# Turning the first two chunks of x on TensorE instead of in the DMA

## The chip, the cores and the metric

The kernel runs on one core of one Trainium2 chip. The metric is the device time of one execution in microseconds (us). The core has five engines that this document names: TensorE (PE in the profile, with PEld for its weight loads), VectorE (DVE), ScalarE (ACT), GpSimd (POOL) and SyncE (SP), whose queue issues almost all DMA transfers.

## What is computed

The input x has 2048 tokens of 640 numbers in bfloat16. A linear attention with 32 heads of 20 numbers (branch a) and a gated feed-forward layer of width 1728 (branch b) are both computed from x, and a gate for each token mixes them:

```python
g = _sigmoid((x * gate_w).sum(-1, keepdims=True))
a = _A_ref(x, A_wqkv, A_w_phi, A_wo)          # heads, softmax features, num / den, @ wo
b = (_silu(x @ w_gate) * (x @ w_up)) @ w_down
return g * a + (1 - g) * b
```

The change concerns only how the first quarter of x reaches the products `x @ w_gate` and `x @ w_up`.

## The kernel before, in words

**Tiling.** The tokens are worked on in four blocks of 512. The 640 columns of x are five chunks of 128. TensorE sums over the partitions, so x is kept transposed in `xT`: chunk, then token, with the 128 columns of a chunk on the partitions. The feed-forward width is cut into 14 tiles k (13 of 128 columns and one of 64); one tile of a block is a group of five matmuls for gate and five for up, 512 tokens wide, one for each chunk. `wg` and `wu` hold the gate and up weights.

**Order.** The code does not issue instructions in the order in which it is written. It hands tasks to a plan (`_Plan`, L241), each with an engine, an assumed cost, what it depends on, a priority and the PSUM banks that it takes and frees. The plan's `run` (L286) simulates time with these figures: whenever an engine is free, the task of the best priority whose dependencies have ended is issued. A load's end is the due time `land` that its call gives. Some tasks of the later stages also have a `hold`, a fixed simulated time before which they do not start (`K_AT`, `Q_AT`, `PRE_AT`, L724 to L727). The result is one fixed instruction order for each engine; on the chip, semaphores make each instruction wait for its data.

**The loads.** `load` (L494) chains all transfers of SyncE's queue in the order of the calls. The first are, L547 to L553: gate weights of chunks 0 and 1 for the tiles k = 0 to 3 (256 KB), x chunks 0 and 1 of the first 512 tokens through the DMA's transpose, the up weights of chunks 0 and 1, gate weights of chunks 2 to 4 for k = 0 and 1, x chunks 2 and 3 and then 4 (transposed), and the rest of the weights for k = 0 to 3. After them come the next columns of gate and up, and the second block of x.

**The head.** TensorE begins with ten 512-column warm-up matmuls on constants (`warm`, L618; instructions at L623), whose results nobody reads. They are chained in front of `ffn_head` (L694), which treats the tiles k = 0 to 3 of the first block in an order by arrival of data: gate for chunks 0 and 1 (eight matmuls), up for chunks 0 and 1 (eight), then chunks 2 to 4 of gate (twelve) and of up (twelve). All these matmuls are issued at L450, in the helper `mms`; copies from PSUM by ScalarE and its other functions are at L460, DMA issues at L478, memsets at L470. ScalarE, VectorE and GpSimd finish each tile (`ffn_tail`: L460, L665, L671). The plan fills the time in which the attention's chain is not ready with further tiles of the feed-forward layer.

Of the kernel before, what the change touches and what calls it, by code (L numbers as in the profile page):

```python
# [6 lines left out]
P = 128  # L7
S_TOK = 2048
D = 640
H = 32  # L10
DH = 20
F_FFN = 1728
NT = S_TOK // P
# [16 lines left out]
NPC_W = 6  # L30
PHI_NH = (6, 6, 6, 6, 6, 2)
ACTF = mybir.ActivationFunctionType
ALU = mybir.AluOpType
AX = mybir.AxisListType
DT = mybir.dt
BF16 = DT.bfloat16
# [204 lines left out]
class _Plan:  # L241
# [11 lines left out]
    def add(self, eng, cost, fn, deps=(), prio=5.0, lat=None, acq=(), rel=(), name=""):  # L253
        t = _Task(eng, cost, fn, deps, prio, self.LAT[eng] if lat is None else lat,
                  tuple(acq), tuple(rel), len(self.tasks), name)
        self.tasks.append(t)
        return t
# [82 lines left out]
def _mm(*cols):  # L340
    return sum(c / 2400.0 + 0.003 for c in cols)


def _build(
# [13 lines left out]
    pe, act, dve, pool, sp = nc.tensor, nc.scalar, nc.vector, nc.gpsimd, nc.sync  # L358
    run = tr.run

    def rowelems(shape):
        r = 1
        for s_ in shape[1:]:
            r *= s_
        return r

    def sb(name, shape, dtype):
        t = nc.alloc_sbuf_tensor(name, list(shape), dtype)
        tr.reg_tensor(t, "sbuf", nc.lookup_mloc(t).addr, rowelems(shape), mybir.dt.size(dtype))
        return t  # L370

    def sbat(name, shape, dtype, at):
        t = nc.alloc_sbuf_tensor_at(name, list(shape), dtype, offset=at)
        tr.reg_tensor(t, "sbuf", at, rowelems(shape), mybir.dt.size(dtype))
        return t

    xT = sb("xT", [P, 5, S_TOK], BF16)
# [33 lines left out]
    base = nc.lookup_mloc(slab).addr  # L411
# [2 lines left out]
    wqT = sbat("wqT", [P, 2 * NPC_W, D], BF16, base)  # L414
    wbd = sbat("wbd", [P, NPC_W, 6, DH], BF16, base + 2 * NPC_W * D * 2)
    wph = sbat("wph", [PC, NPC_W, DH], BF16, base + 2 * NPC_W * D * 2 + NPC_W * 6 * DH * 2)

    ps = nc.alloc_psum_tensor("ps", [P, 8 * 512], F32)
    tr.addr[ps.name] = ("psum", 0, 8 * 512, 4)

    x2 = A_x[0]
# [3 lines left out]
    add = plan.add  # L425
# [4 lines left out]
    def one(b, c0, c1, r0=0, r1=P):  # L430
        return ps[r0:r1, b * 512 + c0:b * 512 + c1]
# [4 lines left out]
    def mms(groups):  # L436

        reads = [g[1] for g in groups] + [g[2] for g in groups]
        writes = []
        seen = set()  # L440
        for g in groups:
            k = (g[0].offset, str(g[0].ap))
            if k not in seen:
                seen.add(k)
                writes.append(g[0])

        def fn():
            last = None
            for o, l, r, st, sp_ in groups:
                last = pe.matmul(o, lhsT=l, rhs=r, start=st, stop=sp_, skip_group_check=True)  # L450
            return last
        run("pe", fn, reads=reads, writes=writes)
# [5 lines left out]
    def actop(o, i, func, scale=1.0):  # L458
        reads = [i] + ([scale] if isinstance(scale, bass.AP) else [])
        run("act", lambda: act.activation(o, i, func, scale=scale), reads=reads, writes=[o])  # L460

    def dveop(fn, reads, writes):
        run("dve", fn, reads=reads, writes=writes)

    def poolop(fn, reads, writes):
        run("pool", fn, reads=reads, writes=writes)

    def memset(t_ap, val, eng):
        eobj = {"pool": pool, "dve": dve}[eng]
        run(eng, lambda: eobj.memset(t_ap, val), reads=[], writes=[t_ap])  # L470
# [3 lines left out]
    def dma(eng, dst, src, transpose=False, keep=False):  # L474
        eobj = tr.engobj[eng]
        reads = [src] if src.tensor.name in tr.addr else []
        writes = [dst] if dst.tensor.name in tr.addr else []
        fn = (lambda: eobj.dma_start(dst, src, transpose=True)) if transpose else (lambda: eobj.dma_start(dst, src))  # L478
        ev = run(eng, fn, reads=reads, writes=writes, semname="dma")
        if keep:  # L480
            out_evs.append(ev)
# [12 lines left out]
    def load(eng, dst, src, land, prio, transpose=False, name="load", cost=0.06):  # L494

        t = add(eng, cost, lambda: dma(eng, dst, src, transpose=transpose), prio=prio, lat=2.0, name=name)
        t.land = land
        t.slack = L_SLACK if land > 13 else 0.0
        t.after = chain.get(eng)
        chain[eng] = t  # L500
        return t
# [7 lines left out]
    wgl = [None] * (NPC + 1)  # L509
    wul = [None] * (NPC + 1)  # L510

    def load_gu(j, eng, land, prio):
        c0, c1 = PIECES[j]
        wgl[j] = load(eng, wg[:, :, c0:c1], gsrc[:, :, c0:c1], land[0], prio)
        wul[j] = load(eng, wu[:, :, c0:c1], usrc[:, :, c0:c1], land[1], prio + 0.1)

    def load_x(bt, prio, *cuts):

        tok = slice(512 * bt, 512 * bt + 512)
        out_ = []  # L520
        for i, (c0, c1, land) in enumerate(cuts):
            out_ += [load("sp", xT[:, c0:c1, tok], x2[tok, c0 * P:c1 * P], land, prio + 0.1 * i, True, "x%d" % bt)] * (c1 - c0)
        return out_
# [13 lines left out]
    xs = [None] * NBT  # L537
    HD = 4
    hw = {}

    def load_head(key, c0, c1, k0, k1, land, prio):
        w, src = (wg, gsrc) if key == "g" else (wu, usrc)
        t = load("sp", w[:, c0:c1, k0 * P:k1 * P], src[:, c0:c1, k0 * P:k1 * P], land, prio)
        for k in range(k0, k1):
            hw[key, c0, k] = t
        return t
    load_head("g", 0, 2, 0, HD, 3.9, -43)  # L547
    xa = load_x(0, -42, (0, 2, 5.25))
    load_head("u", 0, 2, 0, HD, 6.9, -41)
    load_head("g", 2, 5, 0, 2, 7.4, -40.5)  # L550
    xs[0] = xa + load_x(0, -40, (2, 4, 8.8), (4, 5, 9.3))
    wgl[0] = load_head("g", 2, 5, 2, HD, 10.0, -39.5)
    wul[0] = load_head("u", 2, 5, 0, HD, 11.3, -39)  # L553
    load_gu(1, "sp", (12.5, 13.7), -37)
    xs[1] = load_x(1, -36.5, (0, 5, 16.4))
    phi_rows = A_w_phi.rearrange("h e f -> (h e) f")
# [16 lines left out]
    xl = [x_[4] for x_ in xs]  # L573

    zero = add("dve", 0.3, lambda: memset(us[:, 0, 0:2], 0.0, "dve"), prio=-20, name="zero")
    table = add("act", 1.3, lambda: actop(us[:, 1, 0:1], us[:, 0, 0:1], ACTF.Tanh), deps=[zero], prio=-20, name="table")
# [39 lines left out]
    def warm(banks, before):  # L618
        ctx = {}

        def fn():
            for b in banks:
                last = pe.matmul(one(b, 0, 512), lhsT=ones_row[:, 0:P], rhs=ones_row[:, 0:512], start=True, stop=True, skip_group_check=True)  # L623
            return last
        b0, b1 = min(banks), max(banks) + 1
        t = add("pe", 0.427 * len(banks), lambda: run("pe", fn, reads=[], writes=[ps[:, b0 * 512:b1 * 512]]), prio=-10,
                acq=[("bank", ctx, i) for i in range(b0, b1)], rel=[("bank", ctx, i) for i in range(b0, b1)], name="warm")
        t.after = before
        return t
    warm_t = warm((4, 5, 6, 7, 4, 5), warm((0, 1, 2, 3), None))  # L630


    gate_t = {}
# [60 lines left out]
    def ffn_head():  # L694
        tsl = slice(0, 512)
        cs = [{} for _ in range(HD)]
        before = warm_t
        last = {}

        def group(key, c0, c1, parts):  # L700
            nonlocal before
            w = wg if key == "g" else wu

            def fn(ks, cc):
                mms([(one(cs[k][key], 0, 512), w[:, c, P * k:P * k + P], xT[:, c, tsl], c == 0, c == 4) for c in cc for k in ks])
            for ks in parts:
                t = add("pe", _mm(*[512] * (len(ks) * (c1 - c0))), lambda ks=ks: fn(ks, range(c0, c1)),
                        deps=[xs[0][c1 - 1], hw[key, min(c0, 2), ks[-1]]], prio=-5,
                        acq=[("bank", cs[k], key) for k in ks] if c0 == 0 else (), name="head")
                t.after = before  # L710
                before = t
                for k in ks:
                    last[key, k] = t
        group("g", 0, 2, [(0, 1, 2, 3)])
        group("u", 0, 2, [(0, 1, 2, 3)])
        group("g", 2, 4, [(0, 1)])
        group("g", 4, 5, [(0, 1)])
        group("g", 2, 5, [(2, 3)])
        group("u", 2, 5, [(0,), (1,), (2,), (3,)])
        for k in range(HD):  # L720
            ffn_tail(0, k, cs[k], (last["g", k], last["u", k]), 0)
# [372 lines left out]
    pre_q = premult(0, wqT_l, PRE_Q, 0.02)  # L1094
    wq_done[0] = pre_q[-1]
    ffn_head()
    for bt in range(NBT):
        for t in range(4 * bt, 4 * bt + 4):
# [5 lines left out]
    for bt in range(1, NBT):  # L1104
        ks = list(range(K_PAIRS if bt == 1 else 0, NK))
# [74 lines left out]
```

## Time and profile before

| What | Value |
|---|---|
| median of 3 runs | 286.7 us (286.43 to 286.81) |
| the profiled execution | 286.7 us, of which the span of its instructions is 285.0 us |
| first warm-up matmul, first real matmul | 0.84 us, 5.10 us |
| a 512-column matmul of the real work, mean duration of one | 379 to 381 ns; they overlap, the next starts after 0.216 us |
| first weights: issue, landing | 0.80 us, 3.0 us later |
| transposed x chunks 0 and 1: issue, landing | 1.31 us, 3.6 us later |
| busy share of the 16 DMA engines, 3 to 8 us, for each microsecond | 0.96 to 1.27 |
| ScalarE idle before its first copy of the head | 8.3 us, until 10.57 |

Times in the profile count from the start of the span. A line of the timeline gives the start, the length, the engine, the line of the kernel, the instruction with the names of the tiles that it writes and reads, and in brackets how long the engine was idle before it and what ended that. Successive matmuls overlap in the record, so their pace is read from the starts, and the starts of the weight loads are the finest view of it. A queue's line (SPq) shows the issuing of a transfer, not its landing.

### The profile page before, as it was taken

The page shows a single profiled execution, that of the slowest core. Times are in us where ns is not written, and L with a number is a line of the kernel's source. Part 1 is how long each engine was busy: PE and PEld are TensorE (multiplying, and loading weights), DVE is VectorE, ACT ScalarE, POOL GpSimd, SP SyncE. Part 2 cuts the span into 40 slices and gives each one's busy share as a digit, 9 for nine tenths or more (in the row PEclk, how much of TensorE's full clock was granted, in tenths as well). Part 3 has the DMA queues.
Part 4 walks back from the last instruction along what each step waited for, and adds up shares of the span by engine and source line. Part 5 has one row for each costly group of instructions (what it writes and reads, how often), then busy time and mean ns, then how long its engine had stood idle before and what let it go on. Part 6 is the DMA issues. An engine that isn't in the chain of part 4 may idle for free.

```text
span 285.0 us, 4720 instructions
## 1 busy us (share of the span) xinstructions
PE 281.9 (99%) x1816; PEld 143.4 (50%) x1816; DVE 225.8 (79%) x326; ACT 150.2 (53%) x242; POOL 172.4 (61%) x170
## 2 busy tenths in 40 slices
PE   8999999999999999999999999999999999999996
PEld 3445554555554544555455455455555554554544
DVE  1323449998999797997999999999998989982132
ACT  2455655886676564345761655366655454563210
POOL 5099633749478637366498286588888643867100
PEclk9999999999999999999999999999999999999999
DMA  7979998940000000000002344444344544535211
GB/s 169 264 124 232 231 234 121 307 140 0 0 2 0 2 18 0 2 0 18 2 1 54 74 97 92 100 102 97 74 99 98 116 100 96 69 63 115 48 46 64
DMA packets 70431, 24.73 MB, mean 87 GB/s; under 512 B 58569, under 2 KB 70409, under 8 KB 70409
## 3 DMA queue, kind: packets, MB, share of 16 engines
q1 hardware_dynamic: 69753, 24.43, 40.2%
q8 instruction: 14, 0.23, 0.3%
q10 hardware_dynamic: 656, 0.00, 0.1%
q14 instruction: 8, 0.07, 0.1%
HBM read 8.30 MB, written 2.62 MB: 38 GB/s over the span
## 4 chain that ended last, share of the span: by engine, by line
PE 99%; DVE 0%; issue 0%
PE ps L450 97%; PE ps L623 2%; DVE xsb L760 0%
## 5 line engine op out<-in xcount | busy, mean ns | idle before, releaser
L671 POOL TENSOR_TENSOR hT<-hT,us 128x512 bf16<-128x512 bf16 (+1 forms) x56 | 64.0, 1154 | 52.3 <-DVE hT L665 31.9
L983 POOL TENSOR_TENSOR phi<-phi,rc 128x1320 bf16<-128x1320 bf16 x32 | 77.6, 2426 | 23.6 <-DVE rc L977 23.6
L450 PE MATMUL ps<-xT,wg 128*128 128x512 bf16 x280 | 69.6, 381 | 0.0
L450 PE MATMUL ps<-xT,wu 128*128 128x512 bf16 x260 | 64.3, 379 | 0.0
L665 DVE SCALAR_TENSOR_TENSOR hT<-hT,ps 128x512 bf16<-128x512 bf16 (+1 forms) x56 | 37.6, 677 | 23.4 <-ACT hT L460 23.3
L460 ACT ACTIVATE phi<-phi 128x1320 bf16<-128x1320 bf16 x32 | 41.7, 1303 | 22.6 <-DVE phi L962 22.6
L973 DVE TENSOR_REDUCE sm<-phi 128x66 f32<-128x1320 bf16 x32 | 48.2, 1510 | 5.5 <-ACT phi L460 5.5
L460 ACT ACTIVATE hT<-ps 128x512 bf16<-128x512 f32 (+1 forms) x56 | 33.0, 595 | 37.1 <-PE ps L450 36.9
L450 PE MATMUL ps<-wd,hT 128*128 128x512 bf16 (+2 forms) x238 | 50.7, 366 | 0.0
L450 PE MATMUL ps<-wkv,xT 128*128 128x289 bf16 (+2 forms) x240 | 45.6, 343 | 0.0
L460 ACT ACTIVATE us<-ps 128x512 bf16<-128x512 f32 (+1 forms) x56 | 33.2, 597 | 15.5 <-PE ps L450 13.5
L450 PEld LDWEIGHTS ps<-xT,wu 128*128 128x128 bf16 x260 | 25.4, 98 | 30.7
L450 PEld LDWEIGHTS ps<-xT,wg 128*128 128x128 bf16 x280 | 25.9, 98 | 27.3 <-issue 1.5
L450 PEld LDWEIGHTS ps<-wd,hT 128*128 128x128 bf16 x238 | 22.4, 98 | 24.0
L450 PEld LDWEIGHTS ps<-wkv,xT 128*128 128x128 bf16 x240 | 23.1, 97 | 19.4
L950 DVE TENSOR_REDUCE mx<-ps 128x33 f32<-128x660 f32 x32 | 26.5, 830 | 2.9 <-PE ps L450 2.9
L962 DVE TENSOR_TENSOR phi<-mn,ps 128x660 bf16<-128x660 f32 x32 | 26.6, 831 | 0.5
L954 DVE TENSOR_REDUCE mn<-ps 128x33 f32<-128x660 f32 x32 | 26.5, 829 | 0.0
L958 DVE TENSOR_TENSOR phi<-ps,mx 128x660 bf16<-128x660 f32 x32 | 26.4, 825 | 0.0
L460 ACT ACTIVATE xsb<-ps,gs 128x512 bf16<-128x512 f32 (+1 forms) x16 | 11.9, 741 | 27.3 <-PE ps L450 27.2
L450 PE MATMUL ps<-wq,xT 128*128 128x512 bf16 (+1 forms) x160 | 24.3, 299 | 0.0
L450 PE MATMUL ps<-wo,oT 128*128 128x512 bf16 (+1 forms) x160 | 24.2, 299 | 0.0
(52 smaller groups left out, 208.9 us busy)
## 6 DMA issues: line engine op xcount, KB each, us to landing
out_dram<-xsb SPq DMA_DIRECT2D x15, 160.0 KB, 1.8
wd<-in_B_w_down_dram SPq DMA_DIRECT2D x1, 2080.0 KB, 10.1
wg<-in_B_w_gate_dram SPq DMA_DIRECT2D x2, 400.0 KB, 6.1
wu<-in_B_w_up_dram SPq DMA_DIRECT2D x2, 400.0 KB, 6.4
wo<-in_A_wo_dram SPq DMA_DIRECT2D x1, 800.0 KB, 10.6
wg<-in_B_w_gate_dram SPq DMA_DIRECT2D x2, 320.0 KB, 5.2
wu<-in_B_w_up_dram SPq DMA_DIRECT2D x2, 320.0 KB, 5.8
wkv<-in_A_wqkv_dram SPq DMA_DIRECT2D x1, 600.0 KB, 5.0
```

The lines of the kernel that those rows point to most:

```text
L450: last = pe.matmul(o, lhsT=l, rhs=r, start=st, stop=sp_, skip_group_check=True)
L460: run("act", lambda: act.activation(o, i, func, scale=scale), reads=reads, writes=[o])
L623: last = pe.matmul(one(b, 0, 512), lhsT=ones_row[:, 0:P], rhs=ones_row[:, 0:512], start=True, stop=True, skip_group_check=True)
L665: dveop(lambda: dve.scalar_tensor_tensor(out=hap, in0=hap, scalar=1.0, in1=g_, op0=ALU.add, op1=ALU.mult), [hap, g_], [hap])
L671: poolop(lambda: pool.tensor_tensor(hap, hap, u_, ALU.mult), [hap, u_], [hap])
L950: dveop(lambda: dve.tensor_reduce(a, b, AX.X, ALU.max), [b], [a])
L954: dveop(lambda: dve.tensor_reduce(a, b, AX.X, ALU.min), [b], [a])
L958: dveop(lambda: dve.tensor_tensor(o_, a, b, ALU.subtract), [a, mx[:, ctx["st"], :]], [o_])
L962: dveop(lambda: dve.tensor_tensor(o_, a, b, ALU.subtract), [b, mn[:, ctx["st"], :]], [o_])
L973: dveop(lambda: dve.tensor_reduce(a, b, AX.X, ALU.add), [b], [a])
L983: poolop(lambda: pool.tensor_tensor(a, a, b, ALU.mult), [a, r], [a])
```

## The change

Chunks 0 and 1 of the first 512 tokens are no longer loaded with the DMA's transpose. Each is loaded as it lies in memory, 128 tokens on the partitions, by a plain transfer of 128 KB into a new tile `xp`; the two transfers are the first of SyncE's queue. TensorE multiplies each of the four 128x128 pieces of a chunk with an identity matrix, which puts the transposed piece into PSUM as 32-bit numbers; VectorE copies one half and ScalarE the other half into `xT`. GpSimd builds the identity. The first gate load is cut into one piece for each chunk, and the first gate group into two groups of four matmuls. Six warm-up matmuls stay of ten. The due times of the loads up to the tile k = 3 are set earlier by 0.4 to 1.1 us.

```diff
-    load_head("g", 0, 2, 0, HD, 3.9, -43)
-    xa = load_x(0, -42, (0, 2, 5.25))
-    load_head("u", 0, 2, 0, HD, 6.9, -41)
-    load_head("g", 2, 5, 0, 2, 7.4, -40.5)
-    xs[0] = xa + load_x(0, -40, (2, 4, 8.8), (4, 5, 9.3))
-    wgl[0] = load_head("g", 2, 5, 2, HD, 10.0, -39.5)
-    wul[0] = load_head("u", 2, 5, 0, HD, 11.3, -39)
+
+    def load_xp(c, land, prio):
+        return load("sp", xp[:, c, :, :], x2[0:512, c * P:(c + 1) * P].rearrange("(t p) j -> p t j", p=P), land, prio)
+    xp_l = [load_xp(0, 3.4, -43), load_xp(1, 3.9, -42.9)]
+    load_head("g", 0, 1, 0, HD, 4.4, -42.8)
+    load_head("g", 1, 2, 0, HD, 4.9, -42)
+    load_head("u", 0, 2, 0, HD, 5.9, -41)
+    load_head("g", 2, 5, 0, 2, 6.6, -40.5)
+    xs[0] = [None, None] + load_x(0, -40, (2, 4, 7.7), (4, 5, 8.3))
+    wgl[0] = load_head("g", 2, 5, 2, HD, 9.6, -39.5)
+    wul[0] = load_head("u", 2, 5, 0, HD, 10.8, -39)
...
+    def build_ident():
+        memset(ident[:, :], 1.0, "pool")
+        for m, b in ((1, 0), (-1, 0)):
+            poolop(lambda m=m: pool.affine_select(
+                out=ident[:, :], in_=ident[:, :], pattern=[[-m, P]], compare_op=ALU.is_ge, fill=0.0,
+                base=0, channel_multiplier=m), [ident[:, :]], [ident[:, :]])
+    ident_t = add("pool", 0.8, build_ident, prio=-30, name="ident")
...
-    warm_t = warm((4, 5, 6, 7, 4, 5), warm((0, 1, 2, 3), None))
+    warm_t = warm((4, 5, 6, 7), warm((0, 1), None))
+
+    def turn(c, before):
+        ctx = {}
+
+        def fn():
+            mms([(one(ctx[i // 2], P * (i % 2), P * (i % 2) + P), xp[:, c, i, :], ident[:, :], True, True) for i in range(4)])
+        t = add("pe", 0.43, fn, deps=[xp_l[c], ident_t], prio=-10, acq=[("bank", ctx, 0), ("bank", ctx, 1)], name="turn")
+        t.after = before
+        ev = []
+
+        def half(h):
+            return xT[:, c, 256 * h:256 * h + 256], one(ctx[h], 0, 256)
...
+        ev.append(add("dve", 0.36, copy_d, deps=[t], prio=-30, rel=[("bank", ctx, 0)], name="turned"))
+        ev.append(add("act", 0.36, copy_a, deps=[t], prio=-30, rel=[("bank", ctx, 1)], name="turned"))
+        return t, ev
+    turn_t, xe0 = turn(0, warm_t)
+    turn_t, xe1 = turn(1, turn_t)
...
-                        deps=[xs[0][c1 - 1], hw[key, min(c0, 2), ks[-1]]], prio=-5,
+                        deps=(xe[c1 - 1] if c1 < 3 else [xs[0][c1 - 1]]) + [hw[key, c0, ks[-1]]], prio=-5,
...
-        group("g", 0, 2, [(0, 1, 2, 3)])
+        group("g", 0, 1, [(0, 1, 2, 3)])
+        group("g", 1, 2, [(0, 1, 2, 3)])
```

## Prediction

> **What bounds the kernel now.** The profiled execution took 286.7 us, which is also the median of the three runs (286.43 to 286.81). Its span is 285.0 us, so 1.7 us lie around the span, and I keep them. I read the busy times first, then the chain that ended last.
>
> ```profile
> PE 281.9 (99%) x1816; PEld 143.4 (50%) x1816; DVE 225.8 (79%) x326; ACT 150.2 (53%) x242; POOL 172.4 (61%) x170
> ...
> PE 99%; DVE 0%; issue 0%
> ```
>
> The same chain in order of time (start, length, what):
>
> ```profile
> 0.80 0.04 issue
> 0.84 4.43 PE ps L623 x10
> 5.27 277.53 PE ps L450 x1806
> 282.80 0.03 issue
> 282.83 0.35 DVE xsb L760
> ```
>
> TensorE works from 0.84 us to 282.8 us. First come ten warm-up products that nobody reads (L623), then 1806 real ones without a hole. A stage's time falls only if TensorE issues less, issues it faster, or starts its real work sooner. So the timeline of the weight loads (one ahead of each matmul) around the start comes next:
>
> ```profile
> 4.21 0.15 PEld L623 LDWEIGHTS ps<-const-bfloat16-1.0 128*128 128x128 bf16 x1 [0.28 <-issue]
> 5.07 0.15 PEld L450 LDWEIGHTS ps<-xT,wg 128*128 128x128 bf16 x2 [0.70 <-issue]
> 5.49 0.15 PEld L450 LDWEIGHTS ps<-xT,wg 128*128 128x128 bf16 x1 [0.28 <-issue]
> 5.92 0.15 PEld L450 LDWEIGHTS ps<-xT,wg 128*128 128x128 bf16 x1 [0.28 <-issue]
> 6.27 0.75 PEld L450 LDWEIGHTS ps<-xT,wg 128*128 128x128 bf16 x4 [0.20 <-issue]
> 7.13 0.10 PEld L450 LDWEIGHTS ps<-xT,wu 128*128 128x128 bf16 x1
> ```
>
> Steps of 0.43 us (5.49 to 5.92) give way to 0.21 to 0.22 (four loads from 6.27, the next at 7.13): up to about 6.2 us a 512-column matmul takes 0.427 us, afterwards 0.216. The granted clock reads 1.00 in both stretches, so the loads' spacing is the view that shows this. Real work starts at 5.10; 16 matmuls are through when the next group starts:
>
> ```profile
> 7.35 1.89 PE L450 MATMUL ps<-xT,wu 128*128 128x512 bf16 x8
> 9.07 2.75 PE L450 MATMUL ps<-xT,wg 128*128 128x512 bf16 x12
> ```
>
> After 6.2 us the matmuls keep that pace to the end. Hence the rule of this case: one microsecond of earlier start before 6.2 us is worth only half a microsecond at the end.
>
> **SyncE's queue**, since the change reorders it:
>
> ```profile
> 0.80 0.45 SPq L478 DMA_DIRECT2D wg<-in_B_w_gate_dram  x1
> 1.31 1.31 SPq L478 DMA_TRANSPOSE xT<-in_A_x_dram  x1
> 2.69 0.56 SPq L478 DMA_DIRECT2D wu<-in_B_w_up_dram  x1
> 3.29 0.47 SPq L478 DMA_DIRECT2D wg<-in_B_w_gate_dram  x1
> 3.81 2.55 SPq L478 DMA_TRANSPOSE xT<-in_A_x_dram  x2
> 6.40 0.58 SPq L478 DMA_DIRECT2D wg<-in_B_w_gate_dram  x1
> 7.02 0.49 SPq L478 DMA_DIRECT2D wu<-in_B_w_up_dram  x1
> ```
>
> From issue to landing these took 3.0, 3.6, 3.7, 3.7, 3.4 to 4.2, 3.3 and 4.2 us: the first weights are there at 3.8 us, the first two chunks of x at 4.9, the last piece (gate and up columns, `u` chunks 2 to 4) at 11.2.
>
> **The change, part by part.**
>
> *Warm-up.* Four of ten matmuls go: 4 x 0.427 = 1.71 us. The rest end at 0.84 + 6 x 0.427 = 3.40 us.
>
> *Identity.* One memset and two selections on GpSimd, 128x128. The 128x126 rows show 0.21 and 0.35 us each, so 0.9 us in all, from 0.80 to 1.7. Wanted at 3.4. GpSimd's mask building moves from its end at 4.7 to 5.6; its next due work starts at 13.59. Hidden; without that cover, 0.9 us.
>
> *The untransposed loads.* Each brings 128 KB. No row shows a first load in pieces of 256 bytes. Nearest rows: 256 KB of weights in 3.0 us, the transposed 256 KB of x in 3.6; the quickest of any landing is 1.4 (32 KB of output). I take 2.9, near the first weights. Issue costs 0.45 to 0.58; I take 0.5 with the pause. So chunk 0 lands at 0.8 + 2.9 = 3.7 us, chunk 1 at 1.3 + 3.0 = 4.3, the first gate piece (issued 1.8) at 4.8, the second (2.3) at 5.4, `u` at 2.9 + 3.7 = 6.6.
>
> *The queue behind.* Issue times before `u` 2 to 4: 0.45 + 1.31 + 0.56 + 0.47 + 2.55 + 0.58 = 5.92 us. After: 2 x 0.5 + 2 x 0.45 + 0.56 + 0.47 + 2.55 + 0.58 = 6.06, and two more pauses of 0.05. Everything behind is issued about 0.24 us later. Chunks 2 and 3 of x land at 8.2 instead of 8.0, `u` 2 to 4 at 11.45 instead of 11.2.
>
> *Turning.* Four 128-column matmuls for each chunk. Slow 128-column matmuls are not shown; a quarter of 0.427 gives 0.43 us for four, the slow weight load (0.147) 0.59, the fast rows (7.1 us for 80) 0.36. I take 0.5. Chunk 0 is turned from 3.7 to 4.2. The second turn waits on TensorE's own queue for chunk 1, and every real matmul stands behind it: 4.3 to 4.8.
>
> *Copies.* ACT: between 0.32 (128x180) and 0.60 (128x512), about 0.39 for 256 columns. DVE: between 0.35 (128x128) and 0.49 (128x384), about 0.42. Both are otherwise idle there (ACT until 10.57, DVE from 3.65 to 11.20). A matmul's result follows its issue by some 0.2 us (219 ns rows), so chunk 0 is ready at 4.2 + 0.2 + 0.42 = 4.85; chunk 1 at 5.45, under the four slow matmuls of chunk 0. If the second copy had no such cover it would cost 0.6 us. The turns hold four of the eight PSUM banks until then, and the first `up` group, which needs them, starts at 7.1: no wait.
>
> *Start of real work.* The latest of 4.8 (turn of chunk 1), 4.8 (weights) and 4.85: about 4.9 us instead of 5.10. By 6.2 us 3.0 matmuls are done; the other 13 take 2.8 us; the next group starts at 9.0 instead of 9.07. Needed then: x at 9.0 (lands 8.2) and `u` 2 to 4 at 9.0 + 12 x 0.216 = 11.6 (lands 11.45). Both hold, the second narrowly. **Sum: 0.2 / 2 = 0.1 us gained: 286.6 us.**
>
> The ends: with loads of 1.4 us the data wait for the end of the warm-up at 3.40; the quickest turn (0.36), the result's 0.2 and the copy's 0.42 bring the start to 4.4, which gains 0.7 / 2 = 0.35 (286.35). With 3.6 us for either chunk, chunk 1 comes at 4.9, its turn ends at 5.4, the start is 5.5, and 0.2 is lost (286.9). That the real work starts no earlier than today, so that the change moves work without moving time (286.7), lies inside.
>
> **Rivals.**
>
> *The slow pace lasts longer.* Before the change TensorE has no pause between its first matmul and the switch at 6.2 us, 5.4 us later. Afterwards it works until 3.4, then only 1.0 us in the next 1.5. If that break starts the count anew, the switch comes 5.4 us after the first turn (3.7, so 9.1) or after the real start (4.9, so 10.3). Half of 2.9 to 4.1 us is lost, 1.45 to 2.05, less the 0.1: **288.0 to 288.6, say 288.3.** For it: no other row shows the switch passing over a pause. [...] It decides as soon as a pause of about 0.5 us, in two pieces, is held against TensorE.
>
> [...]
>
> *The order behind the head gets a hole.* The plan places every later task by simulated time, and its head now runs about 0.7 us sooner while the holds stay. For it: a list order can tip. Against: in 277 us no hole exists, and filler products abound. Price: between one group of five matmuls (1.08 us) and one GpSimd normalisation (2.43): 287.7 to 289.0, taken at 287.7.
>
> *The full pace arrives sooner.* If the switch is not fixed to 6.2 us and comes at 5.0, it saves 0.6 and with the 0.1 gives 286.0. The three runs differ by 0.38 us, which would be at most 0.76 us of switching time, so this goes beyond what they show.
>
> **How the numbers follow.** About 0.2% (0.57 us) is what a measurement here can tell from no change. Forecast 0.46 (286.35 to 286.9, all within 0.2%); longer slow pace 0.31 (slower); a hole in the order 0.14 (0.10 slower, 0.04 too short to tell); sooner full pace 0.09 (faster). So faster 0.09, same 0.50, slower 0.41. The range runs from 286.2 to 288.6: below it lies most of the 0.09, above it the longer holes, some 0.08.
>
> **What would show it.** Right: warm-up ending at 3.4, chunk loads landing at 3.7 and 4.3, the first `wg` matmul at 4.9, the weight loads' spacing halving near 6.2, the twelve-matmul group at 9.0, and a chain that is TensorE alone afterwards. Wrong: spacing of 0.43 us beyond 7 us (the first rival), a releaser other than PE in the chain behind 10 us (the second), or a second turn that starts after 4.9 because of its load.

## The result and the profile after

The changed kernel took 287.19 us (median of 18 runs, 286.89 to 289.3), the kernel before, beside it, 286.7 us (18 runs, 286.21 to 287.17). The ratio is 1.0032 with a 95% interval of 1.002 to 1.0044: slower, where 0.1 us of gain was forecast. Two things are in that number. Fourteen of the 18 runs lie between 286.89 and 287.47, and four at 288.6 to 289.3, where the kernel before has none. The median moves by 0.5 us; the four late runs carry the ratio further.

The profiled execution took 287.4 us, its span is 285.7. The page's busy times and its chain:

```profile
PE 280.6 (98%) x1787; PEld 143.3 (50%) x1820; DVE 228.4 (80%) x328; ACT 151.0 (53%) x244; POOL 173.2 (61%) x173
...
PE 95%; ACT 1%; DMA 1%; issue 1%; DVE 1%; SPq 0%
```

A trap first: 1787 matmuls are recorded, but 1820 weight loads. 33 matmul records are missing, and the chain has 31 pieces of 0.05 us "issue", nearly all in front of a new piece of TensorE's work, where the kernel before has none. The weight loads are complete (1806 of the real work in both traces), so I read those, at the start:

```profile
3.32 0.40 PEld L454 LDWEIGHTS ps<-ident,xp 128*128 128x128 bf16 x4 [0.66 <-DMA xp<-in_A_x_dram]
4.00 0.35 PEld L454 LDWEIGHTS ps<-ident,xp 128*128 128x128 bf16 x4 [0.27 <-DMA xp<-in_A_x_dram]
4.67 0.13 PEld L454 LDWEIGHTS ps<-xT,wg 128*128 128x128 bf16 x2 [0.33 <-DMA wg<-in_B_w_gate_dram]
...
6.35 0.53 PEld L454 LDWEIGHTS ps<-xT,wg 128*128 128x128 bf16 x3 [0.27 <-issue]
7.00 1.61 PEld L454 LDWEIGHTS ps<-xT,wu 128*128 128x128 bf16 x8
...
10.27 0.98 PEld L454 LDWEIGHTS ps<-xT,wg 128*128 128x128 bf16 x6 [0.37 <-DMA wg<-in_B_w_gate_dram]
...
11.73 2.27 PEld L454 LDWEIGHTS ps<-xT,wu 128*128 128x128 bf16 x12 [0.48 <-DMA wu<-in_B_w_up_dram]
```

The head does what the change says: turns at 3.3 and 4.0 us, real work at 4.67 instead of 5.07, the faster pace from about 6.4. But at 10.27 and 11.73 TensorE waits for weights. Comparing the same weight load in both traces, instruction by instruction, shows where time is gained and lost:

| Instruction | Before, us | After, us | Difference |
|---|---|---|---|
| first real weight load | 5.07 | 4.67 | -0.40 |
| first `up` group | 7.13 | 7.00 | -0.13 |
| gate group after the head | 24.83 | 24.91 | +0.08 |
| weight loads of the products with `eT` | 177.03 | 177.12 | +0.09 |
| end of the last real matmul | 282.80 | 283.52 | +0.72 |

From 25 to 177 us nothing moves. The remaining 0.63 us is lost behind 177 us. Four weight loads there wait for ScalarE (0.19 to 0.54 us, at 200.8, 241.4, 250.1 and 255.3); in the kernel before none does, and the group that waits at 200.79 follows without idle time:

```profile
200.30 0.94 PEld L450 LDWEIGHTS ps<-xT,wu 128*128 128x128 bf16 x5
```

A weight load starts about 0.2 us before its matmul (7.13 and 7.35 us for the first `up` group of the kernel before), so such a wait is not lost in full. The difference between the two traces grows from 0.09 to 0.31 us at 200.8, not at all at 241.4, to 0.50 at 250.1, and by way of a shorter wait at 254.1 to 0.72 at 255.3.

The instruction order differs too. At 14 us two gate groups now run before two `up` groups instead of in turn; the difference between the traces does not grow there. From 177 us on the order changes again and again. Behind the products with `eT` the kernel before (first line) runs a query tile, the changed kernel (second line) a `down` product:

```profile
177.54 1.38 PEld L450 LDWEIGHTS ps<-wq,xT 128*128 128x128 bf16 x10
...
177.63 2.72 PEld L454 LDWEIGHTS ps<-wd,hT 128*128 128x128 bf16 x14
```

### The profile page after: what moved, and what is told of

It reads as the page before. It is cut to its first block, busy times and chain, and to the rows that moved or that the text cites. A ratio compares the mean times of both kernels' runs of the same rounds, so it can differ in the third digit from the quotient of the medians.

```text
span 285.7 us, 4694 instructions
## 1 busy us (share of the span) xinstructions
PE 280.6 (98%) x1787; PEld 143.3 (50%) x1820; DVE 228.4 (80%) x328; ACT 151.0 (53%) x244; POOL 173.2 (61%) x173
## 4 chain that ended last, share of the span: by engine, by line
PE 95%; ACT 1%; DMA 1%; issue 1%; DVE 1%; SPq 0%
PE ps L454 95%; DMA wg<-in_B_w_gate_dram 1%; ACT hT L464 0%; ACT phi L464 0%; ACT us L464 0%; SPq L482 0%; DVE mx L994 0%; DVE mn L998 0%; DVE xsb L804 0%
## 5 line engine op out<-in xcount | busy, mean ns | idle before, releaser
L454 PE MATMUL ps<-xT,wg 128*128 128x512 bf16 x274 | 68.6, 382 | 0.5 <-issue 0.2
L454 PE MATMUL ps<-xT,wu 128*128 128x512 bf16 x256 | 63.6, 379 | 0.4
L454 PE MATMUL ps<-wd,hT 128*128 128x512 bf16 (+2 forms) x230 | 49.8, 366 | 0.4
L454 PE MATMUL ps<-wq,xT 128*128 128x128 bf16 (+1 forms) x156 | 23.6, 297 | 0.2
L454 PE MATMUL ps<-wo,oT 128*128 128x128 bf16 (+1 forms) x157 | 23.7, 297 | 0.2
## 6 DMA issues: line engine op xcount, KB each, us to landing
wd<-in_B_w_down_dram SPq DMA_DIRECT2D x1, 2080.0 KB, 10.2
```

## The experiments

**Theories.** *Order*: the plan places the later tasks otherwise, and that order has holes. *Head*: the changed head itself costs the time. *Pace*, for the late runs: TensorE's pauses in the first 5 us delay the step from 0.427 to 0.216 us for a matmul.

### Order and head apart

`own_order` keeps the change and alters the plan's due times alone, so that behind the head each engine has the order of the kernel before:

```diff
-    load_head("g", 0, 1, 0, HD, 4.4, -42.8)
-    load_head("g", 1, 2, 0, HD, 4.9, -42)
-    load_head("u", 0, 2, 0, HD, 5.9, -41)
+    load_head("g", 0, 1, 0, HD, 5.25, -42.8)
+    load_head("g", 1, 2, 0, HD, 5.25, -42)
+    load_head("u", 0, 2, 0, HD, 6.9, -41)
...
-    wul[0] = load_head("u", 2, 5, 0, HD, 10.8, -39)
+    wul[0] = load_head("u", 2, 5, 0, HD, 11.3, -39)
```

> The changed kernel with later due times for the loads of the head, so that the plan gives every engine exactly the instruction order of the kernel before behind the head; the head's instructions are those of the change. Order theory (the holes behind 177 us come from the other order alone): the holes at 200.8, 250.1 and 255.3 us go, 0.6 us come back, TensorE ends its work 0.1 us later than in the kernel before, time 286.6 to 286.9. Head theory (the changed head itself, its data or its pace, costs the time): it stays at 287.1 to 287.3. Pace theory, for the few runs at 288.6 or more: they stay, about one in five.

`only_order` is the opposite: the kernel before, with the due times of the change and a lower planned cost of the warm-up. No instruction of its head changes.

```diff
-    xa = load_x(0, -42, (0, 2, 5.25))
-    load_head("u", 0, 2, 0, HD, 6.9, -41)
+    xa = load_x(0, -42, (0, 2, 4.56))
+    load_head("u", 0, 2, 0, HD, 5.9, -41)
...
-        t = add("pe", 0.427 * len(banks)
+        t = add("pe", 0.37 * len(banks)
```

> The kernel before, its head untouched, with earlier due times in the plan (and a lower planned cost of the warm-up), so that every engine behind the head has the instruction order of the changed kernel. Order theory: holes near 200, 250 and 255 us appear although nothing else changed, 287.2 to 287.4. Head theory: 286.6 to 286.8, no different from the kernel before. Pace theory: no run at 288.6 or more.

**Measured.** `only_order`: 287.31 us (286.87 to 287.63, 11 runs) beside 286.63, ratio 1.0024 (1.0016 to 1.0033). The order alone costs 0.7 us. Its weight loads show the holes of the changed kernel at the same instructions:

```profile
200.74 0.76 PEld L450 LDWEIGHTS ps<-xT,wu 128*128 128x128 bf16 x5 [0.54 <-ACT us L460]
...
250.07 0.78 PEld L450 LDWEIGHTS ps<-xT,wg 128*128 128x128 bf16 x5 [0.50 <-ACT hT L460]
...
255.22 0.76 PEld L450 LDWEIGHTS ps<-xT,wu 128*128 128x128 bf16 x5 [0.39 <-ACT us L460]
```

`own_order` came out in two bands: six runs at 286.07 to 286.74 and six at 288.16 to 288.93, median 287.45; one late run in five was expected, not one in two. The lower band lies at or below what the order theory gave (286.6 to 286.9), and its profile, of a run of 286.64 us, has no hole. But the head had changed too, as its chain of waits shows:

```profile
4.37 0.62 PE ps L454 x4
4.99 0.02 issue
5.02 0.44 DVE xT L663
5.45 0.14 issue
5.59 277.18 PE ps L454 x1806
```

The first real group starts at 5.59 because it waits for the copy of chunk 1 (5.02), of which it needs nothing: with the later due time the plan gave it a PSUM bank of the second turn. So this run mixed two things. `own_order2` gives the first gate group the due time of the change again, and only the second a late one:

```diff
-    load_head("g", 0, 1, 0, HD, 5.25, -42.8)
-    load_head("g", 1, 2, 0, HD, 5.25, -42)
+    load_head("g", 0, 1, 0, HD, 4.4, -42.8)
+    load_head("g", 1, 2, 0, HD, 6.11, -42)
```

> As own_order, but the first gate group's due time is that of the change, so that its four PSUM banks are not those that the second turn uses. In own_order it was given one of those banks and therefore waited for the copies of chunk 1 as well (real work from 5.6 us instead of 4.7). Order theory: no holes behind 177 us, most runs at 286.3 to 286.6. Pace theory: with the pause as short as in the changed kernel (0.5 to 0.7 us instead of 1.3), the share of runs at 288.0 or more falls from the half seen in own_order to about that of the changed kernel, 4 in 18. If the late runs have to do with the order, they are as many as in own_order.

**Measured.** 286.59 us (286.28 to 286.95, 11 runs, none late) beside 286.65, ratio 0.9999 (0.999 to 1.0007). The group that waited at 200.8 us runs without a hole again:

```profile
200.23 0.96 PEld L454 LDWEIGHTS ps<-xT,wu 128*128 128x128 bf16 x5
```

The two runs are the cross of head and order that they were meant to be: behind the head every engine's sequence of instructions is that of the kernel before in the trace of `own_order2`, and that of the changed kernel in the trace of `only_order`. The head alone gains nothing that can be told from zero, and costs nothing. The order theory stands, the head theory falls.

**Why the order tips.** The plan's own log (its simulated times, not the chip's) has every task behind the head 0.5 us sooner than before. At 177 us the seventh query tile (counting from 0) is next; it may not start before 120.27 + 7 x 8.184 = 177.56. Before, TensorE comes free in the plan at 177.84 and takes it. After, it comes free at 177.34, takes a `down` product instead, and everything behind is dealt anew. In the plan this order has no hole and ends 0.5 us sooner. On the chip it does not, because ScalarE's tasks are planned too cheap (0.49 us for a copy that takes 0.60, 1.2 for an exponential that takes 1.30). The timeline of the changed kernel at the first hole, with ScalarE's rows and TensorE's weight loads:

```profile
198.34 1.29 ACT L464 ACTIVATE phi<-phi 128x1320 bf16<-128x1320 bf16 x1
...
199.65 0.60 ACT L464 ACTIVATE hT<-ps 128x512 bf16<-128x512 f32 x1
200.15 0.59 ACT L464 ACTIVATE us<-ps 128x512 bf16<-128x512 f32 x1
...
200.79 0.76 PEld L454 LDWEIGHTS ps<-xT,wu 128*128 128x128 bf16 x5 [0.54 <-ACT us L464]
```

Four copies and one exponential lie in a row (the two earlier copies at 197.2 and 197.8). At 0.1 us each they are half a microsecond later than planned, which is about the idle time of the weight load that needs the PSUM bank. That the short planned costs are the reason is worked out from these rows; a plan with true costs was not run.

### Pauses and pace

`filled` puts a 256-column warm-up matmul behind each turn of `own_order`; `two_warm` is `own_order` with two warm-ups instead of six:

```diff
     turn_t, xe0 = turn(0, warm_t)
-    turn_t, xe1 = turn(1, turn_t)
+    turn_t, xe1 = turn(1, fill(turn_t, 256))
+    turn_t = fill(turn_t, 256)
```

> own_order with one 256-column warm-up matmul in each of TensorE's two pauses, between the two turns and between the second turn and the first real matmul. If the pauses cost something (pace theory), the runs at 288.6 or more go and the median stays or falls. If the pauses are harmless, it is 0 to 0.1 us slower than own_order, for a filler that ends after the data are there.

> own_order with two warm-up matmuls instead of six, so that TensorE is idle from 1.7 to 3.3 us. Pace theory (an early pause delays the step from 0.427 to 0.216 us for a matmul by a whole period): most runs are 1.2 to 2.0 us above own_order, and the profile shows the spacing of 0.43 us until 8 us or later. If the pace does not depend on earlier work, no change from own_order, and the step stays near 6.3 us.

**Measured.** `filled`: 286.82 us (286.46 to 289.04, 12 runs), one late run where `own_order` had six of twelve. `two_warm`: 288.96 us (288.54 to 289.32, 5 runs): all late, and the spacing of 0.43 us lasts until about 11.1 us.

`before_six` isolates the pause: the kernel before with six warm-ups, without turns, new loads or another order.

```diff
-    warm_t = warm((4, 5, 6, 7, 4, 5), warm((0, 1, 2, 3), None))
+    warm_t = warm((4, 5, 6, 7), warm((0, 1), None))
```

> The kernel before with six warm-up matmuls instead of ten and nothing else changed: same order, same loads, no turning. TensorE pauses from 3.4 to about 5.1 us. Pace theory: most runs are 1.2 to 2.0 us above the kernel before (287.9 to 288.7), without any turn or untransposed load. If the late runs come from the turns or the new loads, this kernel is at 286.6 like the kernel before.

**Measured.** 287.9 us (286.48 to 289.34, 12 runs). Eight of twelve are at 287.49 or more, four look like the kernel before. Its profile is of a run of 287.83 us:

```profile
5.13 0.14 PEld L450 LDWEIGHTS ps<-xT,wg 128*128 128x128 bf16 x2 [2.48 <-issue]
...
8.11 0.15 PEld L450 LDWEIGHTS ps<-xT,wu 128*128 128x128 bf16 x1 [0.28 <-issue]
8.49 0.53 PEld L450 LDWEIGHTS ps<-xT,wu 128*128 128x128 bf16 x3 [0.24 <-issue]
```

The slow spacing lasts until 8.5 us: eight slow matmuls instead of the 2.7 before the switch in the kernel before, 5.3 x 0.211 = 1.1 us, and the run is 1.2 us above it. So a pause with nothing else makes late runs. The pace theory stands, with a correction: not every pause does it. It is a matter of chance. Longer pauses go with more late runs on the whole: counted at the slow pace, TensorE's pauses between the warm-up and the first real matmul add up to about 0.5 us in the profile of the changed kernel (four of 18 runs late), 1.4 in `own_order` (six of 12), 1.8 in `before_six` (eight of 12) and 3.1 in `two_warm` (all five). But in `own_order2` they are 0.8 us and none of 11 runs is late, so the length alone does not settle it.

Does it explain the late runs of the changed kernel itself? `after_again` is that kernel once more, `after_filled` is it with the two fillers (planned at no cost, so that the order stays).

> The changed kernel once more, as the partner of the next one. Order theory and pace theory together: most runs at 286.9 to 287.5, a few (about one in five) at 288.6 or more. If the late runs were a matter of the chip of that day, there are none or nearly only such.

> The changed kernel, its order untouched, with one 256-column warm-up matmul in each of TensorE's two pauses between the turns and the first real matmul. Pace theory: no run at 288.6 or more, all at 286.9 to 287.5. If the late runs have another cause (late data, the order), they come as often as in the changed kernel.

**Measured.** `after_again`: 287.18 us (286.95 to 289.01), one late run of 11, so five of 29 in all. `after_filled`: 287.12 us (286.98 to 287.53), none of 11. That agrees, but none of 11 would not be rare at five in 29. No profile caught a late run of the changed kernel, so for that kernel the pace is argued, from its relatives, and not shown.

### Looking for a version that gains

`two_queues` issues the two first gate pieces from ScalarE's queue, beside x on SyncE's; `two_queues_filled` adds the fillers.

```diff
-    load_head("g", 0, 1, 0, HD, 4.4, -42.8)
-    load_head("g", 1, 2, 0, HD, 6.11, -42)
+    load_head("g", 0, 1, 0, HD, 4.4, -42.8, "act")
+    load_head("g", 1, 2, 0, HD, 6.11, -42, "act")
```

> As own_order2, with the two pieces of the first gate load issued from ScalarE's queue, beside the two x chunks on SyncE's: every load behind them is issued about 1 us sooner. If the late arrival of data in the head is a matter of the place in SyncE's queue, the first real matmul starts at 4.4 to 4.6 us, the last up piece lands before it is needed and the wait of 0.2 to 0.5 us at 11.5 us goes: most runs at 286.1 to 286.4. If the 16 DMA engines are what is full (busy share near 1 from 2.2 us), the pieces land as late as before and the time is that of own_order2.

> two_queues with a 256-column warm-up matmul in each of TensorE's two pauses. Pace theory: no run at 288.0 or more, median at or below that of two_queues by 0 to 0.3 us. If the late runs have another cause, their share is that of two_queues.

**Measured.** `two_queues` has two bands: five runs at 286.08 to 286.2, seven at 287.75 to 288.67. The expected start at 4.5 us did not come. With the weights on a second queue the x chunks land later: the second takes 3.4 us in the chain of waits, 3.0 in `own_order` and 2.6 in the changed kernel. The first turn starts at 3.81 instead of 3.3, real work after 5 us, and TensorE's pauses before it add up to 1.0 us. Its profile is of a run of 288.25 us:

```profile
8.57 0.15 PEld L454 LDWEIGHTS ps<-xT,wu 128*128 128x128 bf16 x1 [0.28 <-issue]
9.00 0.15 PEld L454 LDWEIGHTS ps<-xT,wu 128*128 128x128 bf16 x1 [0.28 <-issue]
9.34 0.96 PEld L454 LDWEIGHTS ps<-xT,wu 128*128 128x128 bf16 x5 [0.20 <-issue]
```

Here the slow spacing ends at about 9.3 us. With fillers, two runs of twelve are late instead of seven; the median is 286.44 us, ratio 1.0005 (0.999 to 1.002). Two fillers do not cover the pauses: in their profile the weight loads are idle for 1.36 us before the first turn (0.66 in the changed kernel), where no filler stands, and for 0.41 before the second. The five lower runs of `two_queues` lie where most were expected (286.1 to 286.4), about 0.5 us below the kernel before, and in the profile with fillers `up` chunks 2 to 4 start at 11.36 us without a wait. So a part of the hope came true, and the late runs take the gain back.

`own2_filled` is `own_order2` with fillers, the best that these parts offer; `act_late` takes it and moves the two loads that TensorE waits for to ScalarE's queue, behind its copies:

```diff
-    wgl[0] = load_head("g", 2, 5, 2, HD, 10.0, -39.5)
-    wul[0] = load_head("u", 2, 5, 0, HD, 11.3, -39)
+    wgl[0] = load_head("g", 2, 5, 2, HD, 10.0, -9.5, "act")
+    wgl[0].hold = 4.95
+    wul[0] = load_head("u", 2, 5, 0, HD, 11.3, -9, "act")
```

> own_order2 (the change with the order of the kernel before) with the same two fillers. Order and pace theory: all runs between 286.1 and 286.9, median 286.4 to 286.6, so at best 0.1% better than the kernel before; the change by itself gives no more than that.

> own2_filled with the two loads that TensorE waits for at 10.3 and 11.5 us (gate for k = 2 and 3, up, both chunks 2 to 4) issued from ScalarE's queue right after its copies of the turned chunks, about 1.5 us sooner. If their place in SyncE's queue makes them late, both waits go and 0.1 to 0.3 us are gained: median 286.2 to 286.4. If the DMA engines are full then, they only delay the other pieces, and the time is that of own2_filled or more.

**Measured.** `own2_filled`: 286.47 us (286.17 to 287.05) beside 286.53, ratio 0.9998 (0.9988 to 1.0007): over all its runs, no version here can be told to be faster than the kernel before. In its profile the switch came early, and TensorE only reached its next wait sooner, 1.03 us of idle time in the weight loads in front of the gate piece at 10.09. `act_late`: 291.09 us (290.64 to 292.85, 6 runs), ratio 1.0163 (1.014 to 1.0186), a clear miss. The 576 KB are issued at 4.9 and 5.4 us, beside chunks 2 to 4 of x. The DMA engines were full there in the changed kernel too (busy share 0.96 from 4.9 to 5.3 us and 1.04 from 5.4 to 5.9; here 1.03 and 1.09), and the chunks now land 6.5 and 7.2 us after their issue, where they took 4.3 and 3.9 in the changed kernel:

```profile
6.42 1.61 PEld L454 LDWEIGHTS ps<-xT,wu 128*128 128x128 bf16 x8
10.42 0.56 PEld L454 LDWEIGHTS ps<-xT,wg 128*128 128x128 bf16 x4 [2.40 <-issue]
12.57 0.13 PEld L454 LDWEIGHTS ps<-xT,wg 128*128 128x128 bf16 x2 [1.59 <-DMA xT<-in_A_x_dram]
12.97 0.15 PEld L454 LDWEIGHTS ps<-xT,wg 128*128 128x128 bf16 x1 [0.28 <-issue]
```

The weight loads are idle twice, 4.0 us together, and TensorE then falls back to the slow spacing until 18.5 us. SyncE issues these chunks at about the same times as in the changed kernel (3.9 and 5.4 us instead of 3.9 and 5.2), and only their landings are later.

## Why the prediction was wrong, point by point

- **Head, right.** Warm-up, identity (0.9 us, hidden) and copies (0.38 and 0.42 us for 0.39 and 0.42) came as worked out. The x chunks landed after 2.5 and 2.6 us instead of 2.9 and 3.0, and the first gate piece, which real work waited for last, at 4.6 instead of 4.8, so real work began at 4.67, not 4.9. The rule that an early microsecond is worth half nearly held: 0.40 us at the start would be 0.20 behind the slow pace, and 0.13 was left at the first `up` group; the pace switched about 0.1 us later than before (at 6.35 instead of 6.27).
- **Landing, wrong by a little.** "Both hold, the second narrowly": `up` chunks 2 to 4 landed at 11.7 us, not 11.45. And the list of loads left out the gate piece for k = 2 and 3: it landed at 10.2, when the six gate matmuls in front of it were already through (weight loads from 8.73, idle 0.37 us before 10.27). These two waits turn the gain of 0.1 us into a loss of 0.1 at 24.9 us.
- **The step that failed: the order behind the head.** The sum put it at nothing, and the rival "the order behind the head gets a hole" got 0.14, because "in 277 us no hole exists, and filler products abound". That shows only that the old order has none. An order made from other due times is another order, and the runs priced it at 0.63 us in the trace, 0.7 us in `only_order`. The price of the rival was also too high: 1.08 to 2.43 us for a hole, where all the waits cost 0.63 together, each being for the rest of a copy and not for a whole group. The sign that the prediction named for it, a releaser other than TensorE in the chain behind 10 us, is there: the chain runs through ScalarE's tasks from 197.2 to 200.8 us.
- **The longer slow pace, half right.** Its price (1.45 to 2.05 us less 0.1) fits the late runs, which are 1.5 to 2.2 us above the others; that these are runs of a longer slow pace is not shown for this kernel. Nor does a run show a count that starts anew: the slow spacing ended 3.4 us after the first real weight load in `before_six`, 4.3 in `two_queues` and 5.5 in `two_warm`, not always after 5.4. It was put as all or nothing; late were five runs of 29, so it hardly moves the median and widens the spread.
- The range held the time. The sign did not.

## What to carry to other kernels

When instructions are placed by a simulated clock, a change of a due time at the start is a change of the order everywhere: compare the two orders before pricing the edit, and separate the two effects by giving the new head the old order and the old head the new one. Warm-up work that ends before the data come is worth less than it seems: in `before_six` a pause of 1.8 us, and nothing else, turned a steady time into one with late runs. And look at all runs: a median of 287.2 hides that one in six takes 289.

## What the runs showed of the hardware

- The switch of pace is not tied to the program: the changed kernel switched at 6.4 us in one profile and at 5.5 in the other (`after_again`). Over the profiles of runs that are not late it came at about 4.6 (`own2_filled`) to 6.4 us, in those of late runs at 8.5, 9.3 and 11.1. What sets the moment, and whether it comes in periods, no run shows.
- The granted clock reads 1.00 in every profile whose slow stretch stands at the start, the late ones too. Only `act_late`, which turned slow again in mid-run, reads less (0.988). Its page has the clock at 8 and 7 tenths in the two slices from 7.3 to 21.8 us and at 9 in all others; the spacing is 0.43 us from 12.6 to 18.5 us and 0.22 afterwards. 0.012 of its span of 290.6 us is 3.5 us, lost in a slow stretch of 6.0 to 7.5 us (the last quick load before it ends at 11.0): by this estimate the slow pace goes with about half the granted clock. `two_warm` has the same spacing from 5.5 to 11.1 us and reads 1.00. In the traces of the kernel before and of the changed kernel the first entry of the clock stands at 6.2 and 6.3 us, next to the switch; for the slow stretch ahead of it, which reads 1.00, there is none. At the start, the spacing of the weight loads must be read.
- Plain matmuls with an identity did not keep the pace from switching: in the changed kernel it switched at 6.4 us although both turns (3.36 to 4.4 us) lie in the 3 us before.
